# One beta row, fewer masks, wider exponentials and an earlier first gate in a two-layer attention and FFN kernel

## The chip, the cores and the metric

The kernel runs on one core of a Trainium2 chip. The metric is the device time of one execution in microseconds (us), lower is better. Five engines matter here: PE (matrix products, with a separate lane PEld for loading weights), DVE (vector), ACT (exponentials and other table functions, and copies), POOL (a slower general engine without access to the accumulators) and SP (issues DMA transfers). Matrix products land in eight accumulator banks of 128 partitions by 512 floats, called `ps`.

## The reference

Two layers, each an attention block A and a feed-forward block B with residuals, share one set of weights. There are 2048 tokens of width 512 (bf16).

```
x = x + A(layernorm(x)); x = x + B(layernorm(x))      # twice, same weights
A: q, k, v = x@wq, x@wk, x@wv        32 heads of 16, tokens in 4 segments of 512
   per segment s, in order:
     a_dot = softmax(q k^T / 4 + causal mask) v       # inside the segment
     a_mem = phi(q) M / (phi(q) z + 1e-6)             # phi(t) = t+1 if t>0 else exp(t)
     o = sigmoid(beta) * a_mem + (1 - sigmoid(beta)) * a_dot
     M += phi(k)^T v ; z += sum phi(k)                # memory for later segments
   result: concat(o) @ wo
B: (gelu(x @ w_gate) * (x @ w_up)) @ w_down           # 512 -> 1792 -> 512
```

`beta` has 32 values, one per head. The causal mask keeps key <= query, so of each 128 x 128 diagonal tile of the scores only a triangle counts.

## The kernel before

The work is cut into eight steps k = 0..7: four segments of layer one and four of layer two. Each has an attention part (class `Att`) and a feed-forward part (class `Ffn`). Everything stays on chip; weights and tokens are loaded once.

**The order of instructions is made by a planner.** The function `order` runs on the host when the kernel is built. It keeps a clock for PE (`ck.pe`) and one for each other engine (`Engine.free`), with a fixed cost for each kind of instruction. PE work waits in a list of `Item`s with a readiness test and a due time; work of DVE, ACT, POOL and SP is posted as jobs with slacks. At each step the loop at the end of `order` takes a visit to the scores, or the next product of an open item, or the ready item with the least due time; where nothing is ready while scores are left to do, it emits a filler product of a tile of ones (`warm`) into a free bank. Fillers do no useful work. The numbers in `POLICY` weigh the choices; a job that may run on DVE, POOL or ACT is posted to several engines and the first to be free takes it. Semaphores keep the data correct, whatever the planner believed.

**PE's three modes.** Dense products use the whole 128 x 128 array, or four column strips of 32 (line 471 rather than 476). Scores use four row strips (line 938), and probability times value uses column strips (line 954).

**Scores.** Each segment has 4 blocks b of 8 heads. A block has two parities (`par`), and for each 4 heads at once. One head's causal scores, 512 queries by up to 512 keys, are packed into rounds of 256 columns: `FULL` lists the four rounds of a parity as (key tile, first query, columns, place in the round), and a ninth, shared round of a block holds the other half tiles of both parities (`PAIRED`, `SHARED`). `DIAG` says how many 64-column half tiles at the front of a round hold a triangle. A visit (`score`) does two rounds into four banks; two exponentials of two banks each (line 1396, 128 x 1024) write the probabilities `pt`, in ten slots; then each round with triangles is masked by an `affine_select` on POOL (line 1343), and the shared round by DVE (line 1353) or POOL (line 1348, two halves). A parity's five slots (its four rounds and the shared one) are then multiplied by the values, in a `flush` item (line 954), and DVE turns and scales the result into `aT`.

**From attention to the gates.** `aT` is multiplied by `wo` and added to `x_sb` (line 1027). `Norm` takes statistics of each of the four 128-token rows on DVE (lines 514, 522), then computes the four scales at once on POOL (lines 527, 532), then normalises each row on DVE (line 544). For the steps listed in `BY_PE` the rows are turned on PE (line 586, each with two half-size fillers before it, line 584, `FILL`) and copied to `xnT`. A gate item needs all four rows of `xnT`: four products of 512 columns, for each of 14 gate tiles. Gates, ups and downs of a step are 168 such products.

**The opening** is written by hand: 15 products of ones, the four token rows, their statistics, four turns (line 596), and the first q and k block (lines 909, 914). `beta` arrives as `beta_bc`, one copy for each partition (line 315), and two exponentials of it stand on ACT ahead of the first copies of turned rows (lines 1202, 1203, then 599).

## Time and profile before

| what | value |
|---|---|
| median of three timed runs | 546.5 us (546.19 to 546.84) |
| the profiled execution's own time | 545.75 us |
| its span from first to last instruction | 544.0 us |
| granted PE clock over the span | 0.999 |
| busy: PE, DVE, ACT, POOL | 531.3, 443.7, 434.7, 305.5 us |
| first dense product, last product | 8.48 us, ending near 540.9 us |

The profiled execution took 1.75 us outside its span, and was 0.75 us faster than the median. Busy times are unions of an engine's instructions. A busy PE may be running fillers, so its busy time alone does not say how much of it was needed. A few per cent of the matmul records are missing from the trace, so counts of products are slightly low. A group line gives the line, engine, operation, tiles, shapes, and count, then the busy time, the mean duration, and the idle time just before such instructions with what ended it.

### The profile page before, as it was taken

Reading aid. Unit: us, or ns where it says so; the run is one execution under the profiler, and the core shown is the slowest. Engines: PE = TensorE matmul, PEld = TensorE weight load, DVE = VectorE, ACT = ScalarE, POOL = GpSimd, SP = SyncE. Lnnn points to the kernel's source line nnn. Section 1 sums busy time; section 2 is a strip of 40 time slices with the busy share of each in tenths; the row PEclk is TensorE's granted clock in tenths of the full one; section 3 lists DMA queues with packets and bytes.
Section 4 is the critical chain, followed back from the end, with each engine's and each line's share of the span. In section 5 each row is a group of like instructions: output and inputs, shape, how many; then the busy total and the mean of one; then the engine's idle time right before and its main releaser. Section 6 shows DMA issues by size and latency. Waiting matters only on the chain.

```text
span 544.0 us, 21276 instructions
## 1 busy us (share of the span) xinstructions
PE 531.3 (98%) x9273; PEld 276.3 (51%) x9334; DVE 443.7 (82%) x816; ACT 434.7 (80%) x540; POOL 305.5 (56%) x359
## 2 busy tenths in 40 slices
PE   8999999999999999999999999999999999999997
PEld 4454555454545444554545555545465456555444
DVE  6998999799988999779987998889586797786342
ACT  5999989988898989989899798996879977920330
POOL 4898786369746788339993468716753265300000
PEclk9999999999999999999999999999999999999999
DMA  8406511610331123310312250221320114100001
GB/s 249 117 13 192 118 20 13 176 33 22 45 56 21 26 40 58 44 40 7 41 32 49 33 72 3 41 32 23 78 52 3 22 21 82 24 3 22 19 0 40
DMA packets 64926, 26.95 MB, mean 50 GB/s; under 512 B 49216, under 2 KB 64832, under 8 KB 64832
## 3 DMA queue, kind: packets, MB, share of 16 engines
q1 hardware_dynamic: 64400, 25.31, 22.6%
q8 instruction: 73, 1.20, 0.9%
q10 hardware_dynamic: 432, 0.27, 0.2%
q14 instruction: 21, 0.17, 0.1%
HBM read 9.71 MB, written 2.10 MB: 22 GB/s over the span
## 4 chain that ended last, share of the span: by engine, by line
PE 88%; DVE 7%; DMA 2%; issue 2%; ACT 0%; ACTq 0%; SPq 0%; DVEq 0%
PE ps L476 46%; PE ps L471 26%; PE ps L938 8%; PE ps L954 7%; DVE st L514 1%; DVE x_sb L1027 1%; DMA beta_bc<-in_A_beta_dram 1%; DVE byq L971 1%; PE ps L586 1%; DVE phiq L745 1%; PE ps L584 1%; DMA phik<-e 0%; DMA amT<-am 0%; DVE xn L544 0%; DVE e L764 0%
## 5 line engine op out<-in xcount | busy, mean ns | idle before, releaser
L1396 ACT ACTIVATE pt<-ps 128x1024 bf16<-128x1024 f32 x288 | 278.9, 1025 | 44.6 <-PE ps L938 41.1
L1343 POOL TENSOR_SCALAR_AFFINE_SELECT pt<-pt 128x256 bf16<-128x256 bf16 (+1 forms) x192 | 107.0, 571 | 118.0 <-ACT pt L1396 112.0
L1092 DVE TENSOR_TENSOR gel_sb<-gel_sb,ps 128x512 bf16<-128x512 bf16 x112 | 75.3, 682 | 33.9 <-PE ps L476 25.0
L476 PE MATMUL ps<-xnT,wu_sb 128*128 128x512 bf16 x287 | 66.8, 379 | 1.4 <-issue 1.1
L476 PE MATMUL ps<-xnT,wg_sb 128*128 128x512 bf16 x261 | 62.6, 379 | 0.9 <-issue 0.5
L764 POOL TENSOR_SCALAR e<-e 128x512 bf16<-128x512 bf16 x37 | 57.9, 1565 | 1.8 <-ACT e L741 0.7
L971 DVE STREAM_TRANSPOSE byq<-ps 128x512 f32<-128x512 f32 x64 | 45.0, 706 | 16.5 <-PE ps L954 15.9
L476 PE MATMUL ps<-wd_sb,gel_sb 128*128 128x512 bf16 (+1 forms) x293 | 56.8, 340 | 1.3 <-issue 1.0
L1348 POOL TENSOR_SCALAR_AFFINE_SELECT pt<-pt 64x1024 bf16<-64x1024 bf16 x40 | 47.8, 1196 | 15.0 <-ACT pt L1396 13.7
L1027 DVE TENSOR_TENSOR x_sb<-x_sb,ps 128x512 bf16<-128x512 bf16 (+1 forms) x68 | 42.8, 640 | 16.3 <-PE ps L476 14.7
L471 PE MATMUL ps<-wd_sb,gel_sb 128*32 128x512 bf16 (+1 forms) x792 | 47.1, 378 | 0.3 <-issue 0.3
L476 PEld LDWEIGHTS <-wu_sb 128*128 128x128 bf16 x301 | 28.2, 98 | 33.8 <-issue 0.7
L471 PE MATMUL ps<-xnT,wg_sb 128*32 128x512 bf16 x700 | 42.4, 380 | 0.0
L514 DVE BATCH_NORM_STATS2 st<-x_sb 128x6 f32<-128x512 bf16 x60 | 40.4, 674 | 0.4 <-DMA x_sb<-in_A_x_dram 0.3
L476 PEld LDWEIGHTS <-wg_sb 128*128 128x128 bf16 x273 | 25.3, 98 | 28.8 <-issue 0.2
L476 PEld LDWEIGHTS <-gel_sb 128*128 128x128 bf16 x306 | 28.3, 98 | 22.7 <-issue 1.1
L954 PE MATMUL ps<-pt,vaug 128*32 128x256 bf16 (+2 forms) x1344 | 34.6, 238 | 0.0
L417 POOL TENSOR_SCALAR kx<-kf,masks 128x512 bf16<-128x512 bf16 x20 | 33.5, 1678 | 1.2
L471 PE MATMUL ps<-xnT,wu_sb 128*32 128x512 bf16 x588 | 34.1, 379 | 0.0
L1151 ACT ACTIVATE gel_sb<-gel_sb 128x2048 bf16<-128x2048 bf16 (+1 forms) x21 | 33.2, 1643 | 0.0
L544 DVE TENSOR_SCALAR xn<-x_sb,mv,rs 128x512 bf16<-128x512 bf16 x58 | 31.3, 592 | 2.2 <-POOL rs L532 1.9
L954 PEld LDWEIGHTS <-vaug 128*32 128x32 bf16 x1344 | 27.8, 97 | 10.4 <-issue 2.2
(147 smaller groups left out, 883.6 us busy)
## 6 DMA issues: line engine op xcount, KB each, us to landing
vz<-vaug SPq DMA_DIRECT2D x14, 136.0 KB, 2.9
wg_sb<-in_B_w_gate_dram SPq DMA_DIRECT2D x8, 224.0 KB, 4.6
wu_sb<-in_B_w_up_dram SPq DMA_DIRECT2D x8, 224.0 KB, 4.3
wd_sb<-in_B_w_down_dram SPq DMA_DIRECT2D x7, 256.0 KB, 4.2
x_sb<-in_A_x_dram SPq DMA_DIRECT2D x3, 512.0 KB, 7.3
out_dram<-x_sb SPq DMA_DIRECT2D x12, 128.0 KB, 1.8
xnT<-xn SPq DMA_TRANSPOSE x40, 2.5
wk_sb<-in_A_wk_dram SPq DMA_DIRECT2D x2, 256.0 KB, 6.0
```

The source lines that it names most:

```text
L471: nc.tensor.matmul(out[r], lhsT=lhsT[:, r], rhs=rhs, start=start, stop=stop, tile_position=(0, 32 * c))
L476: nc.tensor.matmul(out, lhsT=lhsT, rhs=rhs, start=start, stop=stop)
L514: nc.vector.bn_stats(out=self.st6[:, 0, :], in_=x_sb[:, self.tt0 + j, :])
L764: lambda eng: eng.tensor_scalar(out=e[0][:], in0=e[0][:], scalar1=1.0, scalar2=None, op0=ALU.min), summed)
L938: nc.tensor.matmul(ps_all[:, bank, o + c0:o + c0 + n], lhsT=lhsT, rhs=self.q[rows, b, q0:q0 + n], start=True, stop=True, tile_position=(32 ...
L954: nc.tensor.matmul(ps()[32 * j:32 * j + 32, q0:q0 + n], lhsT=va[:, ki * VW + g:ki * VW + g + 32], rhs=pt_all[:, places[i], j, c0:c0 + n], ...
L971: nc.vector.transpose(out=self.byq[:, par, :, :].rearrange("p a c -> p (a c)"), in_=ps()[:])
L1027: ck.dve.post(ck.made(), slack, (0.15 + 0.00104 * (c1 - c0), lambda: nc.vector.tensor_tensor(out=xt, in0=xt, in1=ps()[:, 0:c1 - c0], op=AL ...
L1092: ck.dve.post(ck.made(), NORMAL, (0.683, lambda: nc.vector.tensor_tensor(out=g, in0=g, in1=ps()[:], op=ALU.mult), lambda t: (ps.read(t), e ...
L1343: nc.gpsimd.affine_select(out=view, in_=view, pattern=[[0, 4], [0, n], [1, C]], compare_op=ALU.is_ge, fill=0.0, base=C, channel_multiplier=-1)
L1348: nc.gpsimd.affine_select(out=view, in_=view, pattern=[[0, 4 * TPS], [1, C]], compare_op=ALU.is_ge, fill=0.0, base=0, channel_multiplier=-1)
L1396: nc.scalar.activation(out=pt_all[:, s0:s0 + 2, 2 * p:2 * p + 2, :].rearrange("p r h c -> p h r c"), in_=ps_all[:, pair[0]:pair[1] + 1, :] ...
```

## The change

- `beta` is loaded as one row of 32 values, spread to all partitions by one PE product with a row of ones into the last bank, behind the opening's 15 products; the two exponentials read that bank, and stand on ACT behind the copies of the first two turned rows.
- `FULL`, `DIAG` and the new `ORDER` repack the rounds: each parity has two rounds with two half tiles of triangles, and two with none. `ORDER` places the two so that they fall into one visit, for even and odd blocks; such a pair is masked by one `affine_select` over both slots (128 x 1024). The products of a flush are sorted by key tile.
- Where a visit's four banks are neighbours, one exponential (128 x 2048) replaces two.
- The norm ahead of a feed-forward part works in two groups of two rows: scales, normalisation and turns of rows 0 and 1 start when their statistics are there. The first three gate tiles (`split=3`) are opened on these 256 tokens (four products of 256 columns) and finished by a second item for the other 256.
- The half-size fillers ahead of turned rows go (`fill=0`).
- Nearly all values in `POLICY` are new, so the order of the remaining work and the choice of engines change throughout; the planner's opening times and its cost formulas for masks and exponentials are set anew. The planner's own search loop is rewritten.

```diff
-FULL = [[(0, 64, 256, 0)], [(1, 192, 64, 0), (0, 320, 192, 64)], [(1, 256, 256, 0)], [(3, 448, 64, 0), (2, 320, 192, 64)]]
-DIAG = [1, 1, 0, 2]
+FULL = [[(1, 192, 64, 0), (0, 64, 192, 64)], [(0, 256, 256, 0)], [(1, 256, 256, 0)], [(3, 448, 64, 0), (2, 320, 192, 64)]]
+DIAG = [2, 0, 0, 2]
+ORDER = [[(1, 2, 0, 3), (1, 0, 3, 2)], [(1, 0, 3, 2), (0, 3, 1, 2)]]
...
-    return b, (par,), FULL[i - par * (SHARED + 1)], DIAG[i - par * (SHARED + 1)]
+    n = ORDER[b % 2][par][i - par * (SHARED + 1)]
+    return b, (par,), FULL[n], DIAG[n]
...
-    act_evict=8.464, first_evict=0.965, gate_step=0.061, up_due=-0.553, up_step=0.062, down_due=2.078,
+    act_evict=9.124, first_evict=-9.885, gate_step=0.084, up_due=-2.195, up_step=0.096, down_due=2.6,
...
-    xn_pool=7.037, kb_pool=5.303, cut_pool=1.107, at_pool=10.661, pe_turns=2, gate_due=0.765, shun=0.534,
+    xn_pool=-0.925, kb_pool=0.897, cut_pool=3.307, at_pool=4.83, pe_turns=1, gate_due=0.56, shun=-0.498,
...
+    col_gap=10.405, split=3, join=2, fill=0, x_whole=0, hold=5, early=9.613, starve=0.648, near=-1.526, cap=4,
...
-    beta_bc = cst.tile([P, H], BF16, name="beta_bc")
+    beta_row = cst.tile([1, H], BF16, name="beta_row")
...
-    nc.scalar.dma_start(out=beta_bc[:], in_=A_beta.partition_broadcast(P))
+    nc.scalar.dma_start(out=beta_row[:], in_=A_beta.partition_broadcast(1))
...
     keep_warm(WARM, 0)
+    beta_ps = ps_all[:, BANKS - 1, 0:H]
+    nc.tensor.matmul(beta_ps, lhsT=warm[0:1, :], rhs=beta_row[:], start=True, stop=True)
...
+            self.group = 2 if key[0] == "xnTf" else TPS
...
+                g = j // self.group
+                self.n[g] += 1
+                if self.n[g] == self.group:
+                    self.scales(t, slice(g * self.group, (g + 1) * self.group))
...
-            fill = FILL if self.key in BY_PE else 0
+            fill = pol.fill if self.key in BY_PE and self.key[1] < NK - 1 else 0
...
+                work.sort(key=lambda w: w[2])
...
+                def part(h):
+                    c = slice(L // 2 * h, L // 2 * (h + 1))
+                    return [(Clocks.MM[512] / 2, lambda i=i: product(
+                        ps()[:, c], wg_sb[:, i, ft * P:(ft + 1) * P], self.norm.xnT[:, i, c], i == 0, i == KT - 1))
+                        for i in range(KT)]
...
+                return Item(due, lambda: ck.has(("xnTf", k, 0), ("xnTf", k, 1)) and clear(), part(0), second, kind="gate",
+                            ps=ps, after=("xnTf", k, 1))
...
-    nc.scalar.activation(out=tmp_e, in_=beta_bc[:], func=ACT.Exp)
-    nc.scalar.activation(out=tmp_e2[:], in_=beta_bc[:], func=ACT.Exp, scale=-1.0)
...
     n0.first_turn(0)
     n0.first_turn(1)
+    nc.scalar.activation(out=tmp_e, in_=beta_ps, func=ACT.Exp)
+    nc.scalar.activation(out=tmp_e2[:], in_=beta_ps, func=ACT.Exp, scale=-1.0)
...
+        if len(marks) == 2 and n[0] and n[0] == n[1]:
...
+            ck.pool.post(at, NORMAL, (Port(0.18 + 0.49 * n[0]), lambda: mask(marks[0][0], n[0], 2), both))
...
+        joined = pol.join > (rounds[0][0] > 0) and pairs[1][0] == pairs[0][1] + 1
+        for p, got in enumerate([pairs[0] + pairs[1]] if joined else pairs):
...
                 nc.scalar.activation(
-                    out=pt_all[:, s0:s0 + 2, 2 * p:2 * p + 2, :].rearrange("p r h c -> p h r c"),
-                    in_=ps_all[:, pair[0]:pair[1] + 1, :].rearrange("p h (r c) -> p h r c", r=2), func=ACT.Exp, scale=SCALE)
+                    out=pt_all[:, s0:s0 + 2, h0:h0 + len(got), :].rearrange("p r h c -> p h r c"),
+                    in_=ps_all[:, got[0]:got[-1] + 1, :].rearrange("p h (r c) -> p h r c", r=2), func=ACT.Exp, scale=SCALE)
```

200 lines of the change are left out of this document (119 added, 81 removed).

## The prediction

> **What bounds the kernel now.** I read the page first, then what PE waits for, then where the fillers stand, then the groups of masks and exponentials, then the timeline around the first gates, and last the chain of the opening.
>
> ```profile
> PE 531.3 (98%) x9273; PEld 276.3 (51%) x9334; DVE 443.7 (82%) x816; ACT 434.7 (80%) x540; POOL 305.5 (56%) x359
> PE 88%; DVE 7%; DMA 2%; issue 2%; ACT 0%; ACTq 0%; SPq 0%; DVEq 0%
> ```
> PE holds 98% of the span and 88% of the chain that ended last. What PE itself waited for is small:
>
> ```profile
> PE ps L476 <- issue: 4.3, 27, 0.2
> PE ps L596 <- DVE xn L544: 1.0, 2, 0.7
> PE ps L586 <- DVE byq L971: 0.3, 1, 0.3
> ```
> So the kernel can only get shorter where PE's own time is not needed. The needed part is fixed by the mathematics: 1856 dense products, 288 score rounds, 64 flushes. The change alters none of these counts, nor that 144 score visits each enter and leave the row mode. What is not needed are the fillers. The table by stage of the tile of ones (columns: window; busy time and count on PE, PEld, DVE; clock; transfers) shows where they stand; a filler in column mode counts four times.
>
> ```profile
> 8.00:66.00 58.00, 0.59 (x2) 0.15 (x2) 0.00 (x0) 1.00 0.47 132
> 66.00:82.00 16.00, 6.49 (x45) 2.39 (x45) 0.00 (x0) 1.00 0.15 30
> 82.00:128.00 46.00, 0.38 (x1) 0.10 (x1) 0.00 (x0) 1.00 0.33 71
> 128.00:142.00 14.00, 4.00 (x35) 1.33 (x35) 0.00 (x0) 1.00 0.01 2
> 142.00:474.00 332.00, 0.00 (x0) 0.00 (x0) 0.00 (x0) 1.00 0.23 39
> 474.00:505.00 31.00, 1.54 (x8) 0.58 (x8) 0.00 (x0) 1.00 0.05 17
> 505.00:544.00 39.00, 0.00 (x0) 0.00 (x0) 0.00 (x0) 0.99 0.05 16
> ```
> Busy time overstates pipelined products, so I count and use the pitch. Six in a row took 1.47 us with 0.38 for the last alone, which is (1.47 - 0.38)/5 = 0.218 us each; the half-size ones come 0.11 apart. In 66 to 82 there are 13 whole, 24/4 = 6 in column mode and 8 halves: 19 x 0.218 + 8 x 0.11 = 5.0 us. In 128 to 142: 9 x 0.218 + 0.9 = 2.8. Then 0.9 at 496.6, 0.4 in 8 to 66 and 0.2 in 82 to 128. In all 9.3 us, and none between 142 and 474, where PE always has dense work in store.
>
> The two large stretches are the first and second passage from attention to the gates:
>
> ```profile
> 73.92 0.18 DVE L522 BATCH_NORM_AGGREGATE mv<-st 128x2 f32<-128x6 f32 x1
> 74.50 1.04 POOL L532 TENSOR_TENSOR rs<-ve,mhalf 128x4 f32<-128x4 f32 x1
> 75.55 1.47 PE L476 MATMUL ps<-warm 128*128 128x512 bf16 x6
> 76.43 0.60 DVE L544 TENSOR_SCALAR xn<-x_sb,mv,rs 128x512 bf16<-128x512 bf16 x1
> 80.30 0.60 ACT L462 ACTIVATE xnT<-ps 128x512 bf16<-128x512 bf16 x1
> ```
> The last row's statistics end at 74.1, the scales at 75.5, rows are normalised from 76.4, the last copy ends at 80.9, and the first gate product starts at 81.29.
>
> **The masks.** 192 become 64.
>
> ```profile
> L1343 POOL TENSOR_SCALAR_AFFINE_SELECT pt<-pt 128x256 bf16<-128x256 bf16 x128 | 60.2, 483 | 51.4 <-ACT pt L1396 45.5 <-PE ps L938 4.7
> L1343 POOL TENSOR_SCALAR_AFFINE_SELECT pt<-pt 128x512 bf16<-128x512 bf16 x64 | 47.7, 745 | 66.6 <-ACT pt L1396 66.5
> L1396 ACT ACTIVATE pt<-ps 128x1024 bf16<-128x1024 f32 x288 | 278.9, 1025 | 44.6 <-PE ps L938 41.1 <-POOL pt L1343 2.5 <-POOL kx L417 0.2
> L1151 ACT ACTIVATE gel_sb<-gel_sb 128x2048 bf16<-128x2048 bf16 x14 | 26.6, 1927 | 0.0
> L1151 ACT ACTIVATE gel_sb<-gel_sb 128x1024 bf16<-128x1024 bf16 x7 | 7.5, 1075 | 0.0
> ```
> From 483 and 745 ns, 256 elements cost 262 ns over a base of 221, so 1024 cost 0.221 + 4 x 0.262 = 1.27 us, and 64 of them 81 us against 107.9 before: POOL sheds 27 us. The elements masked are the same; only 128 bases go. On the path: nothing after 142, since PE does not wait for masks. The last flush ends at 474.2 and PE then has 67 us of dense work; `wo` of the last step starts at 486.96, so attention may even slip by some 12 us unpaid.
>
> **The exponentials.** The gelu rows give (1927 - 1075)/1024 = 0.83 ns an element, so a 2048-wide one takes 1025 + 852 = 1.88 us. Two in a row now span 1.94 us (timeline, 128.59 and elsewhere), as they overlap at the seam. A joined visit saves 0.06 us of ACT, not 0.17: 9 us over 144 visits. In the first segment, 18 visits, 1.1 us, and there ACT is at 95% (54.96 of 58 us from 8 to 66), so the first `wo` may come up to 1.1 us earlier. Later it is worth nothing, by the cover above. What it adds is a hold: the first pair of banks comes free 1.94 - 1.02 = 0.92 us later. No row shows PE short of banks; bounds 0 to 0.1 us a visit (the size of one mode change, 0.31 - 0.22 between a dense product and a score), I take 0, the row nearest being PE's 4.3 us of waits in all.
>
> **The half gates and grouped norm.** With two groups, rows 0 and 1 have statistics at 71.9 instead of waiting for 74.1. POOL is in a mask until 72.7, then needs 0.27 and 0.75 (the opening's two-row scale took 754 ns), so normalising can start near 73.9, 2.5 us sooner, and half gates near 77. Three gates give 3 x 4 x 0.109 = 1.3 us of work while rows 2 and 3 follow. Those are not much earlier in themselves: DVE does the same work, POOL pays 2 x (0.27 + 0.75) - 1.37 = 0.7 us more a step (5 us in all, hidden in its 44% idle). But the eight half fillers go (0.9) and the whole chain begins up to 1.1 us earlier with the exponentials. So 1.3 + 0.9 + 1.2 (that and the relief of POOL and DVE) = 3.4 us of the 5.0 saved; bounds 0 (the fillers become idle time) and 5.0. In 128 to 142, 1.3 + 0.6 = 1.9 of 2.8; bounds 0 and 2.8. At 496.6 the 0.9 goes wholly, as down products are in store (they run until 504.4 between turns and gates); bounds 0 and 0.9. Of the small 0.6 I take half, 0.3. Cost: 24 gates of eight half products for four whole, 24 x (8 x 0.109 - 4 x 0.216) = 0.2 us; sorting the flush costs nothing, the products are the same.
>
> **Beta.** The chain shows the load ahead of the first copies:
>
> ```profile
> 1.71 5.38 DMA beta_bc<-in_A_beta_dram
> 7.46 0.98 ACT xnT L599 x2
> ```
> The first turned row is done near 7.1, so the copies can start 0.3 us sooner, and so can everything behind. The exponentials move into ACT's 0.68 us idle before 9.12 (they take 0.23 + 0.21). The added product stands on PE ahead of the first turn at 6.63, so PE now waits for this load: token rows landed 2.7 to 3.0 us after issue, the old beta 5.4, so between 4.4 and 7.1. At 7.1 the turns slip 0.5 us. Bounds -0.5 and +0.5; I take -0.3, as most of the old load's time went to 128 small packets behind the token rows.
>
> **Sum.** -0.3 (opening) - 0.3 (strays) - 3.4 - 1.9 - 0.9 + 0.2 = -6.6 against the profiled 545.75: 539.15. The median of the runs stands 0.75 above that execution, so 539.9, say 540.
>
> **A rule against the change.** Fillers also keep PE's clock up. Here PE opens at half pace (products 0.43 us apart until 3.6 us), then the granted clock is 1.00 in every stretch, across gaps up to 0.9 us. If two passages dropped to half pace for about 2.5 us each, 2 x 1.25 = 2.5 us would come back: 542.5. The Trainium skill, "TensorE: Matmul & The Clock Gate", section on the HAM clock gate, says the array falls back to half clock after an idle window of about 3.4 us. By that rule nothing happens: even with all fillers of 73.8 to 81.3 taken out, scores and flushes come at least every 1.5 us; no run here shows the fall itself. I give it 3 in 100, inside the next case.
>
> **Rivals.** (1) The fillers turn into idle time or into others elsewhere: the gates still wait for DVE (15.8 of 16 us busy in 66 to 82), which must do all four rows first. Then only the opening, the last 0.9 and some 1 to 2 us are left: 543 to 545. Chance 0.20. (2) No measurable change: the passages wait for `aT` and the memory chain instead, and the opening's load eats its gain: 546. Chance 0.05. (3) Slower, by banks: a joined visit pins four neighbouring banks for 0.92 us more, 144 times, and dense products find no free bank while DVE, 82% busy, still reads the others. It decides from 6.6/144 = 0.046 us a visit; at 0.1 us it is 14.4 us, so 554. For it: eight banks, and half gates that hold theirs until rows 2 and 3 come. Against it: four banks are pinned for the same last exponential today, and PE hardly waits. Chance 0.09. (4) Slower, by POOL: the new weights send 2.2 us normalisations and 1.7 us copies to POOL, masks queue behind them, and attention slips by more than its 12 us of cover, of which a slip of 20 would cost 8: 548 after the gains. Chance 0.06.
>
> **How the numbers follow.** The forecast itself (536.5 to 543) has 0.60. Faster by over 0.2% (1.1 us, about what a measurement can tell) is the forecast and rival 1, 0.80; the same 0.05; slower 0.15. The most that can go is 9.3 of fillers, 0.5 of the opening and about 1 of stalls, so below 536 is nearly excluded. The range 536 to 547 leaves out rivals 3 and 4 and a little at the low end.
>
> **What would show it.** Right: fewer than 15 whole fillers behind the opening, none of half size; first gate products 256 wide and starting near 77 in place of 81; 64 masks of 1.2 to 1.3 us; exponentials 2048 wide at 1.88; the first dense product near 8.2; PE with no new idle. Wrong: PE waiting for banks in 142 to 474, idle stretches of over 1 us where the fillers were, or the last flush later than 486.

## The result, and the profile after

The changed kernel takes 549.75 us (median of 6 runs, 548.5 to 550.45) beside 546.4 for the kernel before (545.94 to 546.84): a ratio of 1.0061, with a 95% interval of 1.0048 to 1.0073. It is 3.3 us slower. The forecast of 540.0 was wrong in sign, and the range of 536 to 547 did not hold it. The profiled execution took 549.72 us with a span of 548.0, so the two profiles stand 4.0 us apart in span. In three of the six executions of the changed kernel the mean granted clock of PE was 0.996 or 0.997 (550.25, 550.45 and 549.59 us), in the others and in the profile it was 1.000; what that means stands with the early loads below.

The page of the changed kernel, its busy times and its chain:

```profile
PE 530.3 (97%) x10367; PEld 287.4 (52%) x10419; DVE 452.0 (82%) x824; ACT 429.6 (78%) x457; POOL 278.1 (51%) x242
PE 78%; ACT 8%; DVE 7%; issue 3%; POOL 2%; DMA 1%; ACTq 0%; POOLq 0%
```

PE is about as busy as before in microseconds, but the chain runs through PE for 78% of the span in place of 88%. What was lost is, beside the fillers that are left, time in which PE waits for others. The same table of waits as before, cut to its larger new rows (line waited at, releaser: us in total, times, longest):

```profile
PE ps L498 <- DMA phik<-e: 2.8, 1, 2.8
...
PE ps L498 <- ACT pt L1466: 0.9, 2, 0.6
PE ps L972 <- DVE gel_sb L1146: 0.7, 1, 0.7
...
PE ps L972 <- DVE x_sb L1063: 0.5, 1, 0.5
```

None of these rows has a counterpart before, where no single wait other than the opening's reached 0.4 us. The fillers, by the stage table of the tile of ones (window; busy time and count on PE, PEld, DVE; clock; transfers):

```profile
8.00:66.00 58.00, 6.84 (x48) 2.46 (x48) 0.00 (x0) 1.00 0.57 133
66.00:82.00 16.00, 0.00 (x0) 0.00 (x0) 0.00 (x0) 1.00 0.17 47
...
128.00:142.00 14.00, 0.00 (x0) 0.00 (x0) 0.00 (x0) 1.00 0.01 2
...
474.00:505.00 31.00, 0.00 (x0) 0.00 (x0) 0.00 (x0) 1.00 0.04 11
```

The fillers at both passages to the gates are gone, as forecast, and those near 496 too. But 48 products now stand in 8 to 66, 47 of them in 38 to 50: 7 fillers in column mode (28 products), 19 whole, and one more at 23. At the pitch of 0.218 us the 27 are 5.9 us, beside 9.3 before. So 3.4 us of fillers went. The four rows of waits above come to 4.9 us, more than that.

The largest wait. The timeline of SP's DMA queue in the changed kernel (start, duration, instruction):

```profile
56.06 1.05 SPq L330 DMA_DIRECT2D wu_sb<-in_B_w_up_dram  x2
57.21 1.19 SPq L464 DMA_TRANSPOSE xnT<-xn  x1
58.50 1.22 SPq L464 DMA_TRANSPOSE phik<-e  x1
```

And that of PE, with the idle time before in brackets:

```profile
59.46 0.36 PE L498 MATMUL ps<-gel_sb,phik 128*32 128x128 bf16 x12
62.63 0.76 PE L498 MATMUL ps<-gel_sb,phik 128*32 128x128 bf16 x36 [2.81 <-DMA phik<-e]
```

Twelve products on phi(k) are issued, then PE stands for 2.81 us until the last quarter of phi(k) is turned. That turn was issued by SP at 58.50 and landed 4.1 us later; on SP's queue it stood behind row turns and weight loads that follow one another almost without a gap from 48 us on. New around it are the turns of the third stream's rows (`pe_turns` went from 2 to 1, so those rows are turned by DMA and no longer on PE) between the loads of the gate and up weights. The stage table of the whole kernel, 50 to 66 us, first before, then after (PE, PEld, DVE, ACT, POOL; clock, share of the DMA engines, GB/s):

```profile
50.00:66.00 16.00, 15.79 (x287) 7.97 (x288) 14.46 (x27) 14.95 (x19) 12.42 (x15) 1.00 0.54 142
```
```profile
50.00:66.00 16.00, 13.03 (x374) 7.17 (x367) 12.65 (x25) 12.28 (x14) 13.92 (x9) 1.00 0.94 183
```

The DMA engines went from 0.54 to 0.94 busy, and PE lost 2.76 us of its 16.

The new masks and exponentials, in the groups with each shape apart (count, busy time, mean ns, idle before):

```profile
L1399 POOL TENSOR_SCALAR_AFFINE_SELECT pt<-pt 128x1024 bf16<-128x1024 bf16 x64 | 77.9, 1217 | 96.2 <-ACT pt L1466 90.6
L1466 ACT ACTIVATE pt<-ps 128x2048 bf16<-128x2048 f32 x74 | 139.2, 1881 | 25.8 <-PE ps L972 22.4 <-ACT pt L1466 0.7 <-DVE st L543 0.7
L1466 ACT ACTIVATE pt<-ps 128x1024 bf16<-128x1024 f32 x140 | 135.3, 1026 | 24.1 <-PE ps L972 20.3 <-DVE gel_sb L1146 1.0 <-POOL pt L1404 0.7
```

Their sizes were worked out rightly (1.22 for 1.27 us, 1.88 for 1.88), but only 74 of the 144 visits find four neighbouring banks.

### The profile page after: what moved, and what is told of

Read it like the earlier page. It is cut to its first block, busy times and chain, and to the rows that moved or that the text cites. A ratio compares the mean times of both kernels' runs of the same rounds, so it can differ in the third digit from the quotient of the medians.

```text
span 548.0 us, 23172 instructions
## 1 busy us (share of the span) xinstructions
PE 530.3 (97%) x10367; PEld 287.4 (52%) x10419; DVE 452.0 (82%) x824; ACT 429.6 (78%) x457; POOL 278.1 (51%) x242
## 4 chain that ended last, share of the span: by engine, by line
PE 78%; ACT 8%; DVE 7%; issue 3%; POOL 2%; DMA 1%; ACTq 0%; POOLq 0%
PE ps L503 34%; PE ps L498 30%; PE ps L972 7%; PE ps L990 5%; ACT pt L1466 5%; DVE ab L1015 1%; PE ps L374 1%; DVE x_sb L1063 1%; DVE byq L1007 1%; POOL e L798 1%; DMA phik<-e 1%; DVE st L543 1%; DVE gel_sb L1146 1%; ACT gel_sb L1205 1%; DVE kx L444 0%
## 5 line engine op out<-in xcount | busy, mean ns | idle before, releaser
L1466 ACT ACTIVATE pt<-ps 128x1024 bf16<-128x1024 f32 (+1 forms) x214 | 274.2, 1322 | 50.0 <-PE ps L972 42.7
L1399 POOL TENSOR_SCALAR_AFFINE_SELECT pt<-pt 128x1024 bf16<-128x1024 bf16 x64 | 77.9, 1217 | 96.2 <-ACT pt L1466 90.6
L503 PE MATMUL ps<-xnT,wg_sb 128*128 128x512 bf16 (+1 forms) x296 | 57.6, 337 | 1.3 <-issue 0.6
L498 PE MATMUL ps<-xnT,wu_sb 128*32 128x512 bf16 x912 | 53.3, 379 | 0.0
L503 PE MATMUL ps<-xnT,wu_sb 128*128 128x512 bf16 x209 | 49.5, 379 | 1.3 <-issue 1.0
L498 PE MATMUL ps<-xnT,wg_sb 128*32 128x512 bf16 (+1 forms) x940 | 47.3, 346 | 0.0
L1205 ACT ACTIVATE gel_sb<-gel_sb 128x2560 bf16<-128x2560 bf16 (+1 forms) x21 | 35.8, 1775 | 0.0
L498 PEld LDWEIGHTS <-gel_sb 128*32 128x32 bf16 x964 | 25.0, 97 | 20.2 <-issue 1.3
L990 PE MATMUL ps<-pt,vaug 128*32 128x192 bf16 (+2 forms) x1344 | 34.9, 238 | 0.3 <-ACT pt L1466 0.2
L498 PEld LDWEIGHTS <-wu_sb 128*32 128x32 bf16 x912 | 23.9, 97 | 21.0 <-issue 0.2
```

Source lines behind the costliest of these rows:

```text
L498: nc.tensor.matmul(out[r], lhsT=lhsT[:, r], rhs=rhs, start=start, stop=stop, tile_position=(0, 32 * c))
L503: nc.tensor.matmul(out, lhsT=lhsT, rhs=rhs, start=start, stop=stop)
L990: nc.tensor.matmul(ps()[32 * j:32 * j + 32, q0:q0 + n], lhsT=va[:, ki * VW + g:ki * VW + g + 32], rhs=pt_all[:, places[i], j, c0:c0 + n], ...
L1399: nc.gpsimd.affine_select(out=view, in_=view, pattern=[[0, 4 * rounds], [0, n], [1, C]], compare_op=ALU.is_ge, fill=0.0, base=C, channel_m ...
L1466: nc.scalar.activation(out=pt_all[:, s0:s0 + 2, h0:h0 + len(got), :].rearrange("p r h c -> p h r c"), in_=ps_all[:, got[0]:got[-1] + 1, :] ...
```

## The experiments

In the runs a0 to a4, d0 to d2 and c1 the order of all work is that of the changed kernel, instruction by instruction; only what the diff names differs. Each run is timed beside the kernel before on the same chip. Differences between two runs are taken from their ratios, times 546 us; an interval of a ratio is about 0.1% to each side (0.2% for the repeat of the changed kernel and for the rewritten order with late loads), so a difference of under 0.8 us between two of them says little, and of under 1.2 us where one of those two takes part. The later runs rewrite the order where the text says so.

**The changed kernel again, and its weight loads issued early.**

```diff
-                pieces.append((37.0 + 1.6 * (8 * n + 2 * kt + h), 224, lambda sb=sb, w=w, kt=kt, c=c: load(
-                    sb[:, kt, c], w_view(w)[:, kt, c])))
+                early.append(lambda sb=sb, w=w, kt=kt, c=c: load(sb[:, kt, c], w_view(w)[:, kt, c]))
+                pieces.append((37.0 + 1.6 * (8 * n + 2 * kt + h), 224, lambda: None))
...
-    ck.sp.post(pol.x3_load, pol.piece_slack, (0.57, lambda: load_x(3), last_input))
+    ck.sp.post(pol.x3_load, pol.piece_slack, (0.57, lambda: (load_x(3), ahead(9)), last_input))
```

(`ahead(n)` issues the next n of `early`; two more go with each piece of `wo`.)

> The changed kernel once more, unedited, as the comparison for its variants in this call. In its trace PE waited 2.8 us for a turned phi(k) at 59.6 us, and the 15 opening products of ones all ran 0.43 us apart. Theory A (the time is lost where transfers and engines are later than the written order supposes): the wait for phi(k) is there again within 0.5 us, and the median lies at 549 to 550.5. For the opening I do not know: if the clock's start is set by the code, all 15 products are slow again; if it is chance, this profile shows fewer.

> The 16 loads of the gate and up weights are issued earlier (nine behind the last token load near 21 us, the rest with the four wo loads near 30 to 37 us); every other instruction stands where it stood. Theory A: SP and the transfer engines are free between 40 and 63 us, the wait for the turned phi(k) falls from 2.8 us to under 0.5, and everything behind moves up: 2.3 to 3.0 us less than the changed kernel, 546.7 to 547.5. Rival B (PE is held there by the work behind the transposition, exponentials and statistics, or the slack is eaten later): the wait at 59.6 moves to another instruction and the time falls by less than 1 us.

Unedited: 548.69 us (546.73 to 550.38), ratio 1.0046 (1.0028 to 1.0064). With early loads: 546.69 (546.0 to 547.53), ratio 1.0012 (1.0003 to 1.0021): 1.9 us faster. The wait for the turned phi(k) is gone from the table, and the stage 50 to 66 now reads:

```profile
50.00:66.00 16.00, 15.95 (x400) 8.49 (x393) 15.39 (x30) 14.82 (x17) 13.58 (x9) 1.00 0.29 56
```

PE has its 16 us back and the DMA engines are at 0.29. The turn that PE had waited for now starts on SP's queue at 53.68:

```profile
53.68 1.22 SPq L471 DMA_TRANSPOSE phik<-e  x1
```

That is 4.8 us earlier than the 58.50 of the changed kernel, and it lands in 2.5 us, where the two of that stage took 4.9 and 4.1. Even a landing after 4.9 us would have come at 58.6, ahead of the 59.8 at which PE began to wait, so the place on the queue is what counts first; the turns of rows did not land faster here (median 3.5 us from 50 to 56, for 2.8 in the changed kernel). The times also lie closer together, over 1.5 us and not 3.7. So this wait is a collision of transfers, it costs about 2 us, and its size differs from execution to execution (2.8 and 2.0 us in the two profiles of the changed kernel). As the first comparison gave 549.75 and this one 548.69 for the same kernel, the 2 us are known only to about 1.

The late loads also go with a fall of the granted clock. Over both comparisons, five of the unedited kernel's twelve executions have a mean clock of 0.996 or 0.997; their median is 550.25 us, that of the seven others 548.5. With early loads none of eleven lies under 0.999. The run with two masks below, whose loads are late too, has such an execution in its profile: PE stood for some 2 us up to 60.9 us, waiting for the turned phi(k), and the granted clock was 0.50 from 63 to 65 us. So in some executions the wait is followed by a few microseconds at half clock. Whether the fall lengthens those executions, or a longer wait brings both, no run separates.

**Joined exponentials and wide masks taken apart again**, each in the changed kernel as it was:

```diff
-                nc.scalar.activation(
-                    out=pt_all[:, s0:s0 + 2, h0:h0 + len(got), :].rearrange("p r h c -> p h r c"),
+                for o in range(0, len(got), 2):
+                    nc.scalar.activation(
+                        out=pt_all[:, s0:s0 + 2, h0 + o:h0 + o + 2, :].rearrange("p r h c -> p h r c"),
```
```diff
-            ck.pool.post(at, NORMAL, (Port(0.18 + 0.49 * n[0]), lambda: mask(marks[0][0], n[0], 2), both))
+            ck.pool.post(at, NORMAL, (Port(0.18 + 0.49 * n[0]), lambda: (mask(marks[0][0], n[0], 1), mask(marks[1][0], n[0], 1)), both))
```

> Each of the 74 joined exponentials (1881 ns) is split into two of two banks again; the order of everything else is kept. Rival C (four banks held together cost time): PE gets the first pair of banks 0.9 us sooner and the time falls by 1 us or more. Theory A: the joined form is worth 0.06 us of ACT each, ACT is not the bound after 90 us, so the time moves by -0.3 to +1 us; most likely +0.3.

> Each of the 64 masks over two slots (1217 ns) is split into two over one slot, about 0.7 us each; the order is kept. Rival D (the wide mask holds up DVE instructions beside it: some took 1.64 us in place of 0.7): the stretched DVE instructions get fewer and the time falls by 1 us or more. Theory A: POOL has 49% idle time, two masks need about 0.2 us more, DVE is stretched as long in all; the time moves by less than 0.7 us either way.

Two exponentials: 548.09 (546.56 to 549.09), ratio 1.0035, 0.6 us under the unedited kernel and within the uncertainty. Two masks: 548.64 (547.35 to 549.11), ratio 1.0044, the same. So banks held longer by a joined exponential are not where 3 us went: the difference is 0.6 us with 1.2 to either side, so at most 1.8 us, or 0.024 us a joined visit.

**The fillers left out**, in the kernel before and in the changed one:

```diff
-                product(ps(), warm[:], wide)
```

(In its place the order counts on as if the product had been issued. In the kernel before, the half-size ones ahead of turned rows go too.)

> The kernel before, its written order unchanged, but none of the products that only fill time is issued (the trace of before has 9.4 us of them, 7.8 of it at 66 to 82 and 128 to 142 us). Theory: they stand where TensorE has nothing ready, because the rows of the feed-forward's norm are not there yet. So leaving them out gives their time back only as idle: the time stays within 1 us of before (545.5 to 547.5) and TensorE shows some 8 us more idle at 66 to 82 and 128 to 142 us. Rival: the order, fixed in advance, puts them before work that is ready; then the time falls by 3 to 9 us (537 to 543). Second rival: the granted clock falls in the gaps and the time rises by more than 1 us.

> The changed kernel, its written order unchanged, without its 27 filling products (5.9 us in its trace, 26 of them at 38 to 47 us). Theory: they stand where rows of the third stream's norm are awaited, and what ends last behind them is the turned phi(k) at 59.6 us, which SP's queue sets and not TensorE. So the time stays within 1 us of the changed kernel (547.7 to 549.7 beside 548.7 in the run of the unedited kernel). Rival: they stand before work that is ready: 4 to 6 us faster (543 to 545).

Before: 545.32 (543.73 to 546.11), ratio 0.9981 (0.9971 to 0.9991), so 1.0 us faster. Changed: 547.93 (546.77 to 551.3), ratio 1.0035, 0.6 us under the unedited one, within the uncertainty. In the kernel before, nine microseconds of instructions were taken out and one came back: most fillers stand where PE would wait in any case. For what it would wait is not always a row. In the kernel before, the new waits from 66 to 84 us are for a turned phi(k) (0.9), an exponential (0.7), DVE (0.6) and a mask (0.5), and only at the second passage for a row (0.7). In the changed kernel the largest new row of the table is for exponentials, four waits of 4.2 us in all, 3.9 of them between 36 and 64 us. The stage tables of these two kernels show a second thing. Without fillers in the kernel before, at the first passage (columns as above, clock behind POOL):

```profile
71.00:72.00 1.00, 0.21 (x4) 0.21 (x5) 0.96 (x3) 1.00 (x2) 0.93 (x3) 1.00 0.01 0
...
76.00:77.00 1.00, 0.55 (x27) 0.39 (x27) 1.00 (x3) 1.00 (x2) 0.92 (x3) 1.00 0.06 16
...
79.00:80.00 1.00, 0.98 (x14) 0.46 (x14) 1.00 (x4) 1.00 (x2) 1.00 (x2) 0.60 0.00 0
80.00:81.00 1.00, 0.94 (x11) 0.42 (x5) 0.93 (x3) 1.00 (x3) 0.83 (x3) 0.50 0.00 0
81.00:82.00 1.00, 0.84 (x2) 0.30 (x2) 1.00 (x2) 1.00 (x2) 1.00 (x1) 0.50 0.00 0
82.00:83.00 1.00, 1.00 (x5) 0.40 (x3) 0.44 (x1) 1.00 (x2) 1.00 (x2) 0.70 0.00 0
```

The granted clock fell to half for some 3.3 us here, once more for as long from 137 us on, and in the changed kernel without fillers for some 7 us, from 41.7 to 48.9. This seems to have taken back part of the gain. The twelve executions of the kernel before without fillers differ in their mean clock, and the time goes with it: 543.73 us at 1.000 (one execution), 543.77 and 543.97 at 0.997, 544.69 to 545.98 at 0.993 to 0.994 (five), 545.09 to 546.11 at 0.991 (four). So leaving out the fillers was worth some 2.4 us in the one execution where the clock held, and 1.0 us in the median.

**Beta as a row alone**, in the kernel before, its order unchanged:

```diff
-    nc.scalar.dma_start(out=beta_bc[:], in_=A_beta.partition_broadcast(P))
+    nc.scalar.dma_start(out=beta_row[:], in_=A_beta.partition_broadcast(1))
...
+    beta_ps = ps_all[:, BANKS - 1, 0:H]
+    nc.tensor.matmul(beta_ps, lhsT=warm[0:1, :], rhs=beta_row[:], start=True, stop=True)
```

> The kernel before with beta as a row alone: 64 values loaded once, spread over the partitions by one product with ones, its two exponentials taken from that bank behind the second opening turn; the order behind the opening is before's. Prediction on record: 0.3 us faster (bounds 0.5 faster to 0.5 slower), so 546.1 beside 546.4. Rival: the opening is set by the clock of the 15 products of ones, which rises at another product in each execution, and the beta row alone is worth nothing that the runs can tell (within 0.3 us), or costs the 0.2 us of a product that stands ahead of the turns.

546.22 (545.49 to 546.9), ratio 0.9999 (0.9991 to 1.0008). Nothing, within half a microsecond. The opening depends on something else: the product of ones at which the pace doubles. (The profile's granted clock reads 1.00 there in all runs, so this rise is read from the distance of the products, not from that column.) Opening products of the profile before, of the changed kernel, and of the next run (start, duration, instruction, idle before):

```profile
1.11 4.79 PE L349 MATMUL ps<-warm 128*128 128x512 bf16 x15 [1.11 <-DVE warm L340]
6.63 0.72 PE L596 MATMUL ps<-ident,xn 128*128 128x128 bf16 x8 [0.73 <-DVE xn L544]
```
```profile
1.11 6.30 PE L374 MATMUL ps<-warm 128*128 128x512 bf16 x15 [1.11 <-DVE warm L365]
7.34 0.18 PE L378 MATMUL ps<-beta_row,warm 1*128 1x32 bf16 x1
7.46 1.07 PE L630 MATMUL ps<-ident,xn 128*128 128x128 bf16 x16
9.03 0.60 PE L943 MATMUL ps<-xnT,wk_sb 128*128 128x256 bf16 x4 [0.50 <-ACT xnT L633]
```
```profile
1.11 4.02 PE L381 MATMUL ps<-warm 128*128 128x512 bf16 x9 [1.11 <-DVE warm L372]
6.79 2.03 PE L637 MATMUL ps<-ident,xn 128*128 128x128 bf16 x16 [1.52 <-DVE xn L585]
8.61 1.06 PE L950 MATMUL ps<-xnT,wk_sb 128*128 128x256 bf16 x4
```

Fifteen products of ones took 4.79 us in one profile and 6.30 in the other: they went from 0.43 to 0.216 us apart after the seventh before, and not at all in the changed kernel's profile. There the row's product and the turns begin late (7.46, for 6.63 before), and the first dense product comes at 9.03 for 8.48. That 0.55 us of the difference between the two profiles is chance: the second profile of the unedited changed kernel has its first dense product at 8.44 (5.71 us for the fifteen), and the kernel before with early loads, whose opening is not edited, at 8.74 (6.23 us).

**Nine products of ones in place of 15**, with the early loads:

```diff
-WARM = 15
+WARM = 9
```

> The changed kernel with the sixteen loads of the gate and up weights issued near 21 to 37 us (546.69 by itself, 2.0 us faster than unedited), and 9 products of ones in the opening in place of 15. Theory: the opening's products of ones last 3.2 to 7.0 us by the product at which the clock rises, and with 15 of them the turns of the first rows begin up to 0.7 us behind those rows; with 9 of them (at most 4.2 us) they never do. So 0.2 to 0.6 us faster than 546.69: 546.1 to 546.5. Rival: the clock rises later for want of work, the first turns and dense products run at half speed, and the time is 0.3 to 1 us longer.

546.9 (545.9 to 547.77), ratio 1.0012: the same as with 15. The theory did not hold; the slow products that the rival named are there, the longer time is not. In the last fence above, the turns do begin at 6.79, but the pace has not risen: the sixteen turns take 2.03 us where the changed kernel's took 1.07, and the four dense products 1.06 us for 0.60. What the start gains, the slow pace takes. Half of the twelve executions also have a mean granted clock of 0.996 or 0.997; the profile is not one of them, so it does not show where.

**Whole gates in place of halves**, with the early loads and the order unchanged:

```diff
-                        ps()[:, c], wg_sb[:, i, ft * P:(ft + 1) * P], self.norm.xnT[:, i, c], i == 0, i == KT - 1))
+                        ps()[:], wg_sb[:, i, ft * P:(ft + 1) * P], self.norm.xnT[:, i, :], i == 0, i == KT - 1) if h else silent())
```

(`silent` issues nothing, so the first half's place stays empty.)

> The changed kernel with its weight loads issued near 21 to 37 us (546.69 by itself), the order unchanged, but the first three gate tiles of each stream whole: four products of 512 tokens where the second half stood, nothing where the first half stood. Prediction on record: the halves are worth 3.4 us at the first stream and 1.9 at the second. Theory now: the halves of the changed kernel begin no earlier than before's whole gates did (82.15 against 81.29 us), and what they save is the wait from the second row to the fourth at the first stream alone: whole gates cost 0.5 to 1.5 us (547.2 to 548.2). Rival: the prediction's size holds, 4 us or more (550.7 and up). Second rival: whole gates cost nothing (within 0.3 us), the rows are all there when the first half starts.

550.01 (549.61 to 550.36), ratio 1.0072 (1.006 to 1.0084), 3.3 us slower than with the halves, where 0.5 to 1.5 had been expected. The waits of PE that came with it:

```profile
PE ps L997 <- ACT pt L1480: 1.7, 1, 1.7
PE ps L979 <- ACT pt L1480: 1.2, 2, 1.0
```

In the timeline one wait of 1.0 ends at 80.95 us and the 1.7 at 142.56, each just ahead of gate products; with the halves these two waits are 0.15 and 0.17 us. So the halves had been PE's work while it would have waited for an exponential at the two passages. That is where the forecast had them, but not quite for its reason. It had them start on two rows, near 77 us, while the two others follow. In the profile with early loads the first half starts at 79.76, when all four rows are turned on PE, 0.8 us ahead of the end of the last row's copy (1.2 us at the second passage). The size to set beside the 3.3 us is the forecast's 1.3 and 1.3 for the work of the halves, less 0.2 of cost; this run leaves the rest of its 5.3 us, the half-size fillers and the chain that begins sooner, as it was.

**Masks: halves of them, and none of them**, with the early loads. The first diff is the one of the two masks above; the second issues nothing where `mask` stood.

> The changed kernel with its weight loads issued near 21 to 37 us (546.69 by itself) and each of the 64 wide masks issued as the two masks that it covers. Theory: VectorE's operations with two inputs stand still while GpSimd's mask is under way (1.64 us where 0.69 is usual), and a wide mask of 1.22 us holds them twice as long as one of 0.6; two of the four waits that are left in the trace, 0.72 us at 114 and 0.64 us at 342, come of that and go, so 0.7 to 1.4 us faster: 545.3 to 546.0. Rival: VectorE's delay is hidden but for chance, splitting gives other waits in their place: within 0.5 us of 546.69.

> The changed kernel with its weight loads issued near 21 to 37 us (546.69 by itself), without GpSimd's masks of the diagonal tiles in the score rounds of whole tiles (82 us of GpSimd's time); the causal cut is left out there, so the attention is another one, and all other instructions stand in their places. Theory: all that GpSimd's masks cost is VectorE's standing still beside them and weights waited for by the products behind: 1 to 2 us faster (544.7 to 545.7), with no operation of VectorE at 1.64 us in the divided attention output. Rival: the masks cost nothing on the path (546.2 to 547.2), and what is left against the kernel before comes from elsewhere.

Two masks for each wide one: 545.87 (544.58 to 546.54), ratio 0.9996 (0.9987 to 1.0004), 0.9 us faster than with wide masks. No masks of these rounds: 543.55 (543.09 to 544.2), ratio 0.9954 (0.9943 to 0.9966), 3.2 us faster, more than the 1 to 2 expected. (POOL's masks of the shared rounds stay there.) Here is how a mask costs PE time, in the timeline of the changed kernel:

```profile
112.73 1.16 POOL L1399 TENSOR_SCALAR_AFFINE_SELECT pt<-pt 128x1024 bf16<-128x1024 bf16 x1 [9.93 <-ACT pt L1466]
112.78 1.64 DVE L1015 TENSOR_TENSOR ab<-byq,r 128x512 bf16<-128x512 f32 x1
...
116.39 0.29 PE L972 MATMUL ps<-q,kx 32*128 32x64 bf16 x8 [0.65 <-DVE gel_sb L1146]
```

The product `ab`, divided attention, starts 0.05 us behind the mask and takes 1.64 us, where 0.69 is usual; it ends 0.53 us after the mask. What DVE does next comes later by the 0.95, and two microseconds on PE waits 0.65 us for a bank that DVE reads. With the early loads and two masks, or none, this row of the table of waits is gone. The same group in the kernel before, in the changed one, with two masks and with none (mean ns behind the busy time):

```profile
L979 DVE TENSOR_TENSOR ab<-byq,r 128x512 bf16<-128x512 f32 x32 | 22.7, 708 | 1.1
```
```profile
L1015 DVE TENSOR_TENSOR ab<-byq,r 128x512 bf16<-128x512 f32 x32 | 25.8, 806 | 1.1
```
```profile
L1022 DVE TENSOR_TENSOR ab<-byq,r 128x512 bf16<-128x512 f32 x32 | 23.8, 744 | 1.1
```
```profile
L1022 DVE TENSOR_TENSOR ab<-byq,r 128x512 bf16<-128x512 f32 x32 | 22.9, 717 | 1.1
```

Without these masks DVE is busy 437.4 us in all, with them 453.6, for the same instructions: 16 us of holding. The largest part is not `ab` but the normalised rows `xn` (58 of them, mean 587 ns with masks and 488 without, 5.7 us in all). The kernel becomes 3.2 us shorter; two waits for DVE that go, 0.7 and 0.5 us, are 1.2 of them, and the way of the rest to PE was not followed. Operations that read an accumulator bank (`x_sb<-x_sb,ps`, mean 673 ns after and 670 before, and `byq<-ps`, 707 and 706) did not lengthen. The Trainium skill, "GPSIMD Engine Reference", section Specifications, says that GpSimd shares its way into SBUF with VectorE and contends with VectorE's operations on two SBUF inputs or in a two-port mode; the trace agrees for `ab`, 0.69 to 1.64 us. How much the masks of the kernel before cost it in the same way was not measured. With the loads late, splitting the masks gained nothing (548.64 beside 548.69), so its 0.9 us, known to about 0.7, rest on one order and one pair of runs.

**The order rewritten.** The structure of the change is kept but for two points: two gate tiles are opened in halves rather than three (`split=2`), and one half-size filler stands again ahead of each turned row at the two passages (`fill=1`). The order is written anew by other weights in `POLICY`, from an opening set where the chip has it, and with 0.55 us more allowed for a turned phi(k); the loads are issued 0.9 us apart from 21 us on.

```diff
-    ck.pe, ck.act.free, ck.dve.free, ck.pool.free, ck.sp.free = 10.1, 10.6, 10.5, 8.1, 6.5
+    ck.pe, ck.act.free, ck.dve.free, ck.pool.free, ck.sp.free = 10.7, 11.2, 11.1, 8.1, 6.8
...
-                pieces.append((37.0 + 1.6 * (8 * n + 2 * kt + h), 224, lambda sb=sb, w=w, kt=kt, c=c: load(
-                    sb[:, kt, c], w_view(w)[:, kt, c])))
+                ck.at(21.0 + 0.9 * (8 * n + 2 * kt + h), lambda sb=sb, w=w, kt=kt, c=c: load(
+                    sb[:, kt, c], w_view(w)[:, kt, c]))
...
-turn_later(t, NORMAL, lambda: self.phik[:, :, b * P:(b + 1) * P], lambda: e[0][:], there)
+turn_later(t, NORMAL, lambda: self.phik[:, :, b * P:(b + 1) * P], lambda: e[0][:], there, pol.margin)
```

> The changed structure, with the order written anew by other weights, from an opening set 0.6 us later (its first dense product really starts near 8.3 to 9.0 us, the changed kernel's order reckons with 0.6 less) and with 1.4 + 0.55 us allowed for a turned phi(k) rather than 1.4; the sixteen loads of gate and up weights are issued 0.9 us apart from 21 us on. Theory: the changed kernel lost its gain to waits that its order did not reckon with, so an order that reckons with them has the gain: 543.5 to 545.5, faster than both. Rival: each order of this density slips on other waits, 546 to 548.5, and the change is worth nothing by itself.

542.43 us (542.2 to 543.14), ratio 0.9935 (0.9923 to 0.9947): 3.5 us faster than the kernel before, and more than the theory gave. It has as much in fillers as the changed kernel (10 whole, 14 in column mode and 8 halves: 24 x 0.218 + 8 x 0.11 = 6.1 us, for 5.9), and some stand at the passages again. By the tile of ones:

```profile
38.00:50.00 12.00, 4.14 (x43) 1.48 (x43) 0.00 (x0) 1.00 0.27 56
...
66.00:82.00 16.00, 1.10 (x4) 0.39 (x4) 0.00 (x0) 1.00 0.01 3
...
128.00:142.00 14.00, 2.45 (x18) 0.79 (x18) 0.00 (x0) 1.00 0.01 4
```

The difference is in the waits. Apart from PE's own issue time and the opening, the two largest rows are these, and no wait for phi(k) is among them:

```profile
PE ps L496 <- DMA xnT<-xn: 0.9, 1, 0.9
PE ps L496 <- DMA wv_sb<-in_A_wv_dram: 0.7, 1, 0.7
```

The first gate products of a stream, from the timelines, in us:

| kernel | 1st | 2nd | 4th | last |
|---|---|---|---|---|
| before | 81.29 | 140.27 | 273.84 | 504.42 |
| changed | 82.15 | 142.29 | 278.59 | 508.21 |
| changed, early loads | 79.76 | 140.21 | 276.38 | 505.81 |
| rewritten, early loads | 78.57 | 136.53 | 268.87 | 502.09 |

**What in the rewritten order gives the gain.** Three edits of it, and the early loads in the kernel before as a control:

> The rewritten order with early loads (542.43 by itself), each wide mask issued as the two that it covers, as in the run that gained 0.8 us on the changed kernel's own order. Theory: the wide masks hold VectorE here too (one divided attention output takes 1.69 us in its trace), and some of the waits left in it (0.7 us near 404 and 0.9 us near 461) go: 541.5 to 542.2. Rival: in this order nothing waits for what is held, so within 0.3 us, or up to 0.5 us longer for GpSimd's 10 us of added time.

> The rewritten order (542.43 with early loads) with the sixteen loads issued where the order has them, from 37 us on, as in before and after. Theory: they meet the turns of rows and of phi(k) on SP's queue again; with more room for a turned phi(k) in the order less is lost than the 2.0 us of the changed kernel: 543.0 to 544.4. Rival: the room that the order leaves covers it, within 0.3 us of 542.43.

> The rewritten order with early loads, its weights fitted once more with all gates whole (no half of 256 tokens), the rest of the change as it is. Theory: an order that may be rewritten finds other work for most of the time that the halves save, so they are worth about 1 us and not the 3.3 us of the unchanged order: 543.0 to 544.3, still faster than the kernel before. Rival: the halves are what makes the gain, 3 us or more: 545.4 and up.

> The kernel before with the sixteen loads of gate and up weights issued 0.9 us apart from 21 us on, its order otherwise unchanged. Theory: its trace shows no wait for a turned phi(k) over 0.3 us, so the early loads give it nothing: 545.5 to 546.5. Rival: the rewritten order's 3.5 us are in part the loads': 1 us faster or more (545.0 and below).

The edits are those shown: two masks for a wide one (e1), the loads where before and after have them (e2), `split=0` with all weights fitted again, the half-size fillers gone once more (e3), the loads by `ck.at` in the kernel before (b4).

- Two masks: 542.27 (541.87 to 543.07), ratio 0.9929 (0.9915 to 0.9943). The same as wide masks within the uncertainty.
- Loads late: 545.69 (544.83 to 550.94), ratio 1.0001 (0.9981 to 1.0021), 3.6 us lost, more than expected. Two of its eleven executions (548.44 and 550.94 us) have a mean granted clock of 0.997 and 0.994, the others 0.999 or more. The waits are for the turned rows:

```profile
PE ps L495 <- DMA xnT<-xn: 1.9, 2, 1.3
...
PE ps L490 <- DMA xnT<-xn: 1.0, 1, 1.0
```

- All gates whole: 548.1 (547.08 to 548.52), ratio 1.0031 (1.0019 to 1.0042), 5.2 us lost against 1 expected. The rival was right, though the order is another one here, and its waits are for DVE at several places, so how much of the 5.2 is the halves' own stays open.

```profile
PE ps L965 <- DVE gel_sb L1139: 1.0, 2, 0.7
PE ps L613 <- DVE q L481: 0.9, 1, 0.9
PE ps L491 <- DVE xnT L481: 0.8, 1, 0.8
PE ps L983 <- DVE x_sb L1056: 0.6, 1, 0.6
```

- Loads early in the kernel before: 546.18 (545.24 to 546.92), ratio 0.9998 (0.9989 to 1.0007). Nothing. So the early loads mend a fault of the change and are no gain by themselves.

Taken together, with half gates, early loads and an order that keeps clear of the transfers the change is worth 3.5 us. Without the half gates, or with the loads late, that gain is gone in the orders tried. One rival stands untested: no run wrote the order of the kernel before anew in the same way, so how much of the 3.5 us such an order would give without the change is not known. Against its being the new order alone stands the run with whole gates, which had its weights fitted too and was slower than the kernel before.

## Why the prediction was wrong

- **What bounds the kernel.** PE's work is the same before and after, as said, and fillers are time not needed for it. But "the kernel can only get shorter where PE's own time is not needed" was read too simply: leaving all fillers out gained 1.0 us of 9.3, and 2.4 in the one execution in which the clock held. The prediction did tie the gain to rows that come sooner; but behind the fillers PE also waited for exponentials, DVE and a turned phi(k). The "4.3 us of waits" that it read from the row `issue` are for the most part no waits: the changed kernel has 4.6 us there in the profile with 10367 PE records and 0.6 in the one with 10419, as many as weight loads, and the profile before lacks 61 records by the same count.
- **The sum's failing step** is that it has no term for the new order. It priced each edit within the order of before and let the rest run as it ran, which puts "nearly all values in `POLICY` are new", a row of the change's list, at nothing without a reason. In its place the runs show transfers colliding at 50 to 64 us, about 2 us (the early loads); 5.7 us of new fillers at 38 to 47; and DVE held by POOL at several places. With the loads early and the order written anew the same change, but for the two points named, stands at -3.5 us and not at +2.5 to +3.3. By that measure 6 to 7 of the 9.9 us between forecast and result belong to the order and its loads, and the 3 that are left to the sizes below. That the new fillers come of the third stream's rows, now turned by DMA, is argued from the order; no run turned these rows on PE again, and in the run without fillers PE waited there for exponentials. Rival 1 named the fillers ("into others elsewhere") with 543 to 545 and 0.20. No rival named the collision.
- **Half gates and grouped norm** (-3.4 and -1.9). The work of the halves was worth its price or more, 3.3 us in an unchanged order for 2.6 less 0.2. What failed is the early start that the other 2.7 us hang on. The first gate product came at 82.15 and not near 77 in the changed kernel, at 79.76 with the early loads, at 78.57 in the rewritten order. With the early loads, normalising did begin at 74.41, close to the 73.9 worked out and 2.0 us sooner than before; but the order has DVE take the statistics of all four rows first, and PE turn all four, before the first half.
- **The 0.9 near 496** went, as said.
- **Masks.** The size was near, 1.22 us for 1.27. The masks of these rounds shed 30.0 us (107.9 to 77.9) where 27 was worked out; that POOL as a whole shed 27.4 is luck, as its other work changed too. "On the path: nothing" was wrong: leaving the masks out gave 3.2 us, with DVE held 16 us less, and the wide ones cost 0.9 us more than narrow ones in one order and nothing to be measured in two others.
- **Exponentials.** 1.88 us as worked out, in 74 visits of 144. Held banks, rival 3, cost at most 1.8 us, not 14; taking 0 was near.
- **Rival 4**, POOL, was right in that POOL costs time on the path, wrong in the way: attention did not slip (the last flush's last products begin at 471.65 for 473.89 before), and it is DVE that stood still beside the masks.
- **Beta** (-0.3, bounds 0.5 to either side): 0.0 with half a microsecond to either side, so the -0.3 is neither shown nor excluded.
- **The clock.** The prediction gave a fall of the clock 3 in 100 and said that by the rule it cited nothing would happen even without fillers. The clock did fall: in the kernel before without fillers the granted clock fell to 0.5 for 3.3 us after a stretch of eight microseconds in which PE's longest gap was 0.9 us. The Trainium skill, "TensorE: Matmul & The Clock Gate", section "Why this matters for your kernels", advises against gaps of over some 3 us; by that alone the clock should have held, and the measurement decides. In the changed kernel too the mean clock was 0.996 or 0.997 in five of twelve executions, and these were slower by 1.75 us in the median. So the clock can have a part in its slowness, behind the wait for phi(k) where one profile shows it, and not at the two passages. It is not the main cause: the executions at 0.999 to 1.000, 548.5 in the median, are still slower than the kernel before.
- **What would show it wrong** named the sign that came: idle stretches of over 1 us. The longest, 2.8 us, came over 10 us ahead of where the fillers had been. The signs for right came in part: 64 masks of 1.22 us and exponentials at 1.88, but 20 whole fillers, and 7 in column mode, where fewer than 15 were to be left, and the first gate at 82.15.

## What to carry to other kernels

Where an order is written in advance and PE is full, a change that makes the plan denser is paid in waits that the plan does not reckon with. So price what moves, and transfers above all: ask of each DMA turn which loads stand ahead of it on its queue and on the engines when it is issued. And try the same structure under another order before judging it: here the changed kernel ran at 549.75 us, at 546.69 with its loads early, and at 542.43 with an order written anew and two small points changed.

## What the runs showed of the hardware that was not expected

- The turn of phi(k) by DMA landed in 2.5 us in the stage with the DMA engines at 0.29, and two of them in 4.1 and 4.9 us at 0.94. The turns of rows show no such difference (median 3.5 us at 0.29 and 3.1 at 0.94, from 50 to 66), so the load of the engines alone does not set it.
- The rise of PE's pace in the opening is not tied to a count of products: it came after 7 of 15 products of ones in the profile before, after all 15 in the changed kernel, and with 9 of them only near 10.2 us, in the middle of the dense products. The Trainium skill, "TensorE: Matmul & The Clock Gate", section on the HAM clock gate, says that the window of activity is free-running, some 3.4 us long; that the rise differs from execution to execution agrees with it, but it came from 2.9 to some 6 us after the first of fifteen products, and no run here shows the window itself.
- The clock falls without a long gap: see the fence on fillers, where PE was at 0.21 in one microsecond. In the five from 74 to 79 us it was busy for 0.29, 0.65, 0.55, 0.69 and 0.77, and the clock fell in the next. The longest gap in all eight was 0.9 us.
- VectorE's division of the attention, started 0.05 us behind a GpSimd mask, ended half a microsecond after it (1.64 us for 0.69), while its reads of accumulator banks kept their length.
